# A new order of operations for a long-convolution block with a feed-forward network: FFN products between the first products of the inverse's second stage

## The chip, the cores and the metric

The kernel runs on one core of a Trainium2 chip. Its engines run side by side, each through a list of instructions of its own: TensorE (PE) multiplies matrices, VectorE (DVE) and ScalarE (ACT) work elementwise, GpSimd (POOL) and SyncE (SP) mostly issue transfers (DMA). The metric is the device time of one execution in microseconds; lower is better.

## The reference

With x of 2048 rows by 640 channels, xn is its layernorm. One branch multiplies a short convolution of k (four taps) by v, convolves the result along the rows with a filter as long as the sequence (by FFT, padded to 4096), adds a skip term and multiplies by xn. The other branch is a feed-forward network (FFN) with 1728 hidden units. Cut to what matters:

```python
kv = k_shift * v                                 # k_shift: 4-tap causal convolution of k
y = irfft(rfft(kv_pad) * rfft(kf_pad))[:S]       # long convolution, per channel
s = xn * (y + kv * ssm_D)
h = gelu(xn @ w1 + b1)                           # 640 -> 1728
g = silu(h @ w2 + b2)                            # 1728 -> 640
out = x + s * g
```

## The kernel before, in words

The FFTs are matrix products in two stages, and between the stages the data goes through DRAM to change which index lies across the partitions.

The program is a list of 713 named operations. A class `Plan` collects them, and `emit` issues them in the order of the string `ORDER` (from line 693). An engine runs its instructions in that order. A token such as `f2_14_1/N@6.0` names an operation (`f2_14_1`), optionally the engine or form (`/A` ACT, `/D` DVE, `/G` POOL, `/S` SP; `/N` splits each product in two of 64 columns), and the buffer slots it takes (`@6.0`: PSUM slot 6, then slot 0 of another pool). PSUM has eight slots. Semaphores between the engines follow from which memory an instruction reads and writes, one instruction at a time.

The names that matter here:

- `xl`, `Kl`, `w1l`, `w2l`, `kl`, `vl`: loads of x, the filter, the weights, k and v, on SP's queue. `wu`: warming products. `ws`: the sine tables.
- `bn`, `rs`, `xn`: layernorm of a tile of 128 rows. `xt` transposes it on PE, `xe` evicts it. `gt`, `gte` transpose the table for the end.
- `f1_c_r_ft`: first FFN product of row chunk c and block ft of the hidden layer (line 435), `ge_...` its Gelu on ACT (line 439). Block 13 is only half wide: `f1h_c` (line 450) and `geh_c` (line 456). `f2_i_h`: half h of the second product of tile i, fourteen products over the blocks in turn (line 476); tile 15 has three parts. It reads the chunk i // 4. `si_i` is its Silu (ACT, line 489), `gx_i` multiplies it into xn (DVE, line 493).
- `kv`: the short convolution and the product with v, on DVE (lines 522 to 531).
- `K1`, `K1r` and `U1`, `U1r`: first stage of the forward FFT of filter and data, `Ke`, `Ker`, `Ue`, `Uer` their evictions, `Ks`, `Us` the stores to DRAM (line 368), four of each.
- `KL`, `UL`: loads of the eight blocks of the second stage (lines 548, 550). `K2`, `U2`, `X2`: its products, `Kf`, `Uf` the evictions. `pr`, `pq`: products of the spectra on DVE. `i1`, `i1r`: first stage of the inverse (lines 604, 632), `ie`, `ir` its evictions, `cs` the store of a block (line 644).
- `cl_r`: load of a block for the inverse's second stage (line 656). It needs all eight `cs` to have landed. `i2_i`: its product for tile i (line 664). `ym_i` multiplies it into xn (DVE, line 668), `ad_i` adds x, `os_i` stores the tile.

Chunk 0 and 1 of the FFN run first, beside K1 and kv; f2 of tiles 0 to 7 beside U1; then f1 of chunks 3 and 2 beside the second stage and i1; f2 of tiles 8 to 11 around the end of i1; f2 of tiles 12 to 15 between the i2. Gelu and Silu need different tables on ACT, and `emit` puts a table load with a small probe (line 686) ahead of an activation whose table is not the one loaded.

Of the kernel before, what the change touches and what calls it, by code (L numbers as in the profile page):

```python
# [694 lines left out]
skl bn3 ws1 wu5@3 bn1 rs1 w1l3 K1_12@4.0 K1_13@6 K1_15@0 bn0 kl0 Ke_13/A wu3@2 ws0 xn2 wu1@3 rs0 xn3 Ke_12/A xt2@6.0  # L695
gt1@7 b1c xe2/D xt3@2 xn1 gt0@3 xe3/A xn0 xt1@6 sm1 xt0@4 xe1/A f1_0_1_1@5.0 xe0/D sm2 f1_0_1_0@2 bn4 f1_0_0_7@6
gte0/D ge_0_1_1 f1_0_0_8@4 bn5 ge_0_1_0 ge_0_0_7 Ke_15/A f1_0_1_2@5 bn7 f1_0_0_5@3 ge_0_1_2 gte1/D ge_0_0_8 one1 bn6
K1_4@0.2 ge_0_0_5 K1_5@6 f1_0_0_0@2 Ke_4/A Ke_5/D rs2 f1_0_0_6@5 ge_0_0_0 sm3 K1_6@0 ge_0_0_6 K1r_1@2 one0 Ke_6/D
# [1 line left out]
xt5@1.1 ge_0_1_4 f1_0_0_1@2 xe5/A xt4@3 kv0_1m@1 xt7@6 xt6@7 xe7/A f1_0_0_11@4 xe6/A kv0_1a f1_0_0_4@5 xe4/A  # L700
f1_0_1_3@1 ge_0_0_10 f1_1_0_5@6.1 ge_0_0_1 kv0_2m@1 ge_0_0_4 ge_0_1_3 K1_14@2 ge_1_0_5 K1r_3@0 kv0_2a f1h_1@7 Ke_14/A
f1_0_0_12/N@5 Ker_3/A bn12 f1_1_0_9/N@6 ge_0_0_11 Ks_3 bn13 vl0 ge_0_0_12 f1_1_0_8/N@2 w2l1 ge_1_0_9 vl1 kv0_3m@1 w2l0
geh_1 f1h_0@3 ge_1_0_8 K1_8@0.2 K1_10@4 kv0_3a K1_9@6 geh_0 f1_1_0_11@2 Ke_8/A bn14 f1_1_0_0@3 Ke_10/A bn15 f1_1_0_2@0
Ke_9/A Da rs4 K1_2@4.0 ge_1_0_2 K1_11@6 f1_0_0_3@1 Ke_11/D ge_1_0_0 f1_1_0_4@0 ge_1_0_11 kv1_1m@1 ge_0_0_3 K1r_0@6
ge_1_0_4 K1r_2@2 f1_1_0_10@1 Ker_2/A xn13 kv0_4 f1_1_0_6@0 Ks_2 ge_1_0_10 kl2 Ker_0/A f1_1_0_3@2 kv1_0@0 ge_1_0_6
f1_1_0_12@3 Ke_2/A kv1_1a ge_1_0_3 K1_1@6 K1_0@0 Ke_1/A K1_3@4 f1_1_0_7@2 kv1_2m@1 xl3 Ke_3/A f1_1_0_1@6 ge_1_0_12
kv1_2a f1_0_0_2@7 ge_1_0_1 f2_3_1@4.0 ge_1_0_7 xn12 kv1_3m@1 Ke_0/A ge_0_0_2 Ks_0 f2_3_0 kv1_3a kl3 vl3 vl2 kv1_4
U1_0@2.2 si_3 U1_1@0 f2_6_0@6.1 Ue_1/A gx_3 xn14 Ue_0/A kv2_0@1 U1_2@4 U1_3@0 Ue_2/A U1r_0@2 kv2_1m@0 f2_6_1 Ue_3/A
kv2_1a xt14@4.1 f2_1_0@0.0 xe14/A KL7@0 Uer_0/A kv2_2m@0 si_6 Us_0 U1_7@4.0 U1_5@2 KL2@1 kv2_2a Ue_7/A f2_1_1 KL1@4
Ue_5/A gx_6 kv2_3m@0 f2_0_0@6.1 si_1 KL0@2 kv2_3a U1_4@4 U1r_1@2 U1_6@0 Uer_1/A kv4_1m@0 f2_0_1 kv2_4 Ue_4/A xt12@2  # L710
si_0 xn15 xe12/D Ue_6/A kv4_0@1 kv4_1a Us_1 KL3@5 gx_0 f2_7_1@4.1 U1_8@6.2 U1_11@2 xt15@0 gx_1 xt13@1 xe15/D f2_7_0
xe13/A kv4_2m@0 Ue_8/A kv4_2a Ue_11/A f2_5_0@0.0 kv4_3m@0 si_7 kv4_3a ss gx_7 U1_10@6 kv4_4 U1r_2@2 Ue_10/A U1_9@4
f2_5_1 bn8 Ue_9/A kv3_0@0 Uer_2/A kv3_1m@1 K2_0_0@6 K2_1_0@4 si_5 Us_2 f2_2_0@2.1 kv3_1a Kf_0_0/A kv3_2m@1 Kf_1_0/A
kv3_2a U1_15@0.0 U1_14@6 Ue_15/A f2_2_1 kv3_3m@1 Ue_14/A kv3_3a kv3_4 f1_3_0_7@4.0 si_2 bn9 U1_12@0 U1_13@6 Ue_12/A
U1r_3@2 Ue_13/D f1_3_0_4@5 Uer_3/A bn11 K2_2_0@0 K2_3_0@6 Us_3 f1_3_0_5@2 bn10 f1_3_0_12@3 ge_3_0_4 Kf_2_0/D rs3
ge_3_0_7 f1_3_0_0@5 ge_3_0_5 ge_3_0_12 xn8 xn11 K2_7_0@0 ge_3_0_0 xt8@4.0 f1_3_0_9@2 Kf_3_0/A xe8/D xn9 K2_2_1@4 UL0@6
ge_3_0_9 xt11@3 Kf_2_1/D UL1@3 xt9@6 Kf_7_0/A UL2@8 f1_3_0_3@7 UL6@9 xe11/D UL3@10 xe9/D KL6@7 K2_0_1@4 ge_3_0_3
K2_1_1@0 xn10 K2_3_1@2 Kf_0_1/A xt10@6 Kf_3_1/D f1_3_0_1@7 Kf_1_1/A gx_2 K2_7_1@4 xe10/D X2_0@2 ge_3_0_1 gx_5 U2_0_0@0
Kf_0_2/A Kf_7_1/D f2_4_0@6.1 Uf_0_0/A Uf_0_2/D pq_0_1@2 U2_1_0@4 pq_0_0 U2_0_1@0 Uf_1_0/A f2_4_1 Uf_0_1/D sx/D
pr_0_0@3 U2_1_1@2 si_4 U2_2_0@4 X2_1@0 pr_0_1@0 Uf_1_1/A f1_2_0_6@6.1 Uf_2_0/D f1_2_0_11@7 UL4/G@2 Uf_1_2/D ge_2_0_6  # L720
i1_0@2.4 Kf_1_2/D ge_2_0_11 pq_1_0 f1_2_0_3@6 ie_0_0/A pq_1_1 pr_1_1@1 ie_0_1/A i1r_0@0.2 f1h_2@7 ir_1_0/D ir_0_1/A
ir_1_1/A pr_1_0@0 U2_2_1@4 ir_0_0/A X2_6@2 ge_2_0_3 U2_6_0@0 Uf_2_1/D Uf_6_2/A KL4@4 f1_2_0_0@6 Kf_6_2/A geh_2
pr_2_1@2 i1_1@2.4 Uf_6_0/A f1_2_0_10@7 ie_1_0/D ie_1_1/A U2_6_1@0 ge_2_0_0 X2_2@2 Uf_6_1/D ge_2_0_10 cs_1 U2_3_0@4
f1_2_0_9@6 Uf_3_0/A Kf_2_2/D Uf_2_2/D X2_4@0 ge_2_0_9 X2_3@4 pq_2_0@3 Kf_4_2/A pq_2_1 U2_3_1@2 Kf_3_2/A pr_2_0@0
f1_3_0_8@7 Uf_3_2/A Uf_3_1/A pq_3_1 f1_3_0_6@6 KL5@1 pq_3_0 Uf_4_2/A pr_3_0@1 ge_3_0_8 i1r_1@4.2 ge_3_0_6 K2_6_0@0
UL5/G@3 ir_3_0/D f1_2_0_2@7 ir_2_0/D ir_2_1/A ir_3_1/A pr_3_1@3 Kf_6_0/A i1_2@4.2 ge_2_0_2 UL7@5 f1_3_0_2@6 ie_2_0/D
ie_2_1/A K2_4_0@0 pq_4_1@0 U2_4_0@2 Kf_4_0/A K2_6_1@4 cs_2 Uf_4_0/D f1_2_0_4@7 Kf_6_1/A cs_0 i1_3@0.2 ge_3_0_2
pr_6_0@2 K2_4_1@4 ie_3_1/A f1_2_0_5@6 gx_4 Kf_4_1/D ie_3_0/A f1_3_0_11@2 ge_2_0_5 cs_3/S pr_6_1@1 ge_2_0_4 X2_5@0
ge_3_0_11 U2_4_1@4 Kf_5_2/D K2_5_0@6 Uf_4_1/A f1_2_0_8@3 Uf_5_2/D Kf_5_0/A pq_5_1 i1_6@0.4 pr_4_0@3 ge_2_0_8
f1_2_0_1@2 ie_6_1/A ie_6_0/D U2_7_0@6 ge_2_0_1 pq_5_0 U2_5_0@4 K2_5_1@0 pq_4_0 Uf_5_0/A f1_2_0_7@3 pr_4_1@1 Kf_5_1/A  # L730
f1_2_0_12@2 Uf_7_0/D ge_2_0_7 i1r_2@4.0 ge_2_0_12 pq_6_0@2 U2_7_1@6 ir_4_1/D ir_4_0/A X2_7@2 ir_5_0/A ir_5_1/D
Uf_7_1/A i1_4@4.0 Kf_7_2/D pq_6_1 Uf_7_2/A f2_11_0@6.0 ie_4_1/A pq_7_1 pq_7_0 pr_7_0@0 ie_4_0/A U2_5_1@2 cs_4/S
pr_7_1@1 i1r_3@0.4 Uf_5_1/A f2_11_1 ir_6_0/A pr_5_0@3 ir_7_0/A ir_7_1/D i1_7@2.0 ir_6_1/D si_11 pr_5_1@2 cs_6/S
# [47 lines left out]
```

## Time and profile before

| | |
|---|---|
| median of 3 runs | 183.24 us (182.97 to 183.44) |
| the profiled execution | 184.05 us, span 182.3 us |
| PE, DVE, ACT, POOL busy | 175.0, 160.9, 138.5, 22.6 us |
| ACT table loads for Gelu and Silu | 8, 10.3 us |
| DMA | 50.64 MB, mean 278 GB/s |

The span runs from the program's first instruction to its last; the rest of the execution's time lies around it. A row of the timeline or of the chain begins with its start and its length in us; then come engine, line, operation, out<-in and the number of instructions taken together, and in brackets the idle time before it and what ended it. PEld is the loading of weights into PE, SPq an issue in SP's queue.

### The profile page before, as it was taken

The numbers are of one execution on the slowest core, as the hardware profiler recorded it, in microseconds if no ns is written. First come the engines' busy times: TensorE is split into PE (matmuls) and PEld (weight loads), VectorE is DVE, ScalarE is ACT, GpSimd is POOL, SyncE is SP. The second block draws the span as 40 slices with busy tenths as digits, with TensorE's granted clock in tenths as the row PEclk, the third lists the DMA queues.
The fourth block names the chain that finished last, engine by engine and source line by source line (L and its number), as shares of the span: only waits on it lengthen the run. The fifth ranks groups of instructions, "written<-read, shape, count | busy, mean of one in ns | idle before, by whom it ended". The sixth has DMA issues, their size and how long they took to land.

```text
span 182.3 us, 5182 instructions
## 1 busy us (share of the span) xinstructions
PE 175.0 (96%) x2192; PEld 99.9 (55%) x2192; DVE 160.9 (88%) x252; ACT 138.5 (76%) x201; POOL 22.6 (12%) x52
## 2 busy tenths in 40 slices
...
GB/s 187 411 415 403 199 367 407 334 425 432 409 309 403 417 358 397 153 287 76 222 340 367 172 141 158 148 325 377 148 4 88 206 287 132 416 405 392 66 189 144
DMA packets 19417, 50.64 MB, mean 278 GB/s; under 512 B 1729, under 2 KB 13506, under 8 KB 17986
## 3 DMA queue, kind: packets, MB, share of 16 engines
...
## 4 chain that ended last, share of the span: by engine, by line
PE 81%; DVE 8%; ACT 7%; issue 1%; ACTq 0%; DVEq 0%
PE ps L435 30%; PE ps L476 30%; PE ps L349 4%; PE ps L604 4%; PE ps L563 4%; PE ps L413 3%; PE ps L664 2%; DVE xn L668 2%; ACT v L181 2%; DVE stats L381 2%; ACT L686 1%; ACT k L181 1%; PE ps L360 1%; PE ps L450 1%; DVE w L238 1%
## 5 line engine op out<-in xcount | busy, mean ns | idle before, releaser
L476 PE MATMUL ps<-w,hT 128*64 128x320 bf16 (+4 forms) x644 | 65.0, 293 | 0.0
L435 PE MATMUL ps<-xnT,w 128*128 128x512 bf16 (+2 forms) x300 | 61.2, 362 | 0.5 <-ACT sl L489 0.2
L476 PEld LDWEIGHTS <-hT 128*64 128x64 bf16 (+3 forms) x644 | 45.3, 105 | 17.4 <-issue 3.9
L435 PEld LDWEIGHTS <-w 128*128 128x128 bf16 (+1 forms) x300 | 26.4, 99 | 28.5 <-issue 6.2
L181 ACT CAST st<-ps 128x1024 bf16<-128x1024 f32 x36 | 35.0, 1014 | 3.4 <-PE ps L360 1.8
L439 ACT ACTIVATE hT<-ps,b1f 128x512 bf16<-128x512 f32 (+1 forms) x57 | 35.0, 665 | 1.2 <-PE ps L435 1.0
L489 ACT ACTIVATE sl<-ps 128x640 bf16<-128x640 f32 (+2 forms) x18 | 11.6, 647 | 24.0 <-PE ps L476 19.4
L529 DVE TENSOR_TENSOR lat<-lat 128x2560 bf16<-128x2560 bf16 (+1 forms) x15 | 18.4, 1225 | 0.5
L526 DVE TENSOR_TENSOR lat<-k,lat 128x2560 bf16<-128x2560 bf16 (+1 forms) x15 | 18.3, 1218 | 0.2
L181 ACT CAST k<-ps 128x1024 bf16<-128x1024 f32 (+2 forms) x19 | 16.2, 878 | 2.6 <-PE ps L563 1.5
L181 ACT CAST v<-ps 128x1024 bf16<-128x1024 f32 (+2 forms) x18 | 14.5, 839 | 0.4 <-PE ps L563 0.4
L668 DVE TENSOR_TENSOR xn<-ps,xn 128x640 bf16<-128x640 f32 x16 | 12.6, 819 | 2.2 <-PE ps L664 2.0
L493 DVE TENSOR_TENSOR xn<-xn,sl 128x640 bf16<-128x640 bf16 (+2 forms) x18 | 8.0, 448 | 7.3 <-ACT sl L489 7.2
L181 DVE CAST k<-ps 128x1024 bf16<-128x1024 f32 (+2 forms) x14 | 11.8, 857 | 2.3 <-PE ps L563 0.9
L381 DVE BATCH_NORM_STATS2 stats<-x 128x6 f32<-128x320 bf16 x32 | 13.7, 470 | 0.0
L686 ACT ACT_TABLE_LOAD x8 | 10.3, 1283 | 0.1
L396 POOL TENSOR_SCALAR rstd<-mv 128x4 f32<-128x4 f32 (+1 forms) x5 | 1.3, 257 | 69.2 <-DVE mv L382 69.2
L181 ACT CAST lat<-ps 128x1024 bf16<-128x1024 f32 (+2 forms) x12 | 9.4, 826 | 0.2 <-PE ps L604 0.2
L604 PE MATMUL ps<-st,I 32*64 32x512 bf16 x256 | 8.8, 380 | 0.1
L332 PE MATMUL ps<-hT 128*128 128x512 bf16 x24 | 7.5, 477 | 1.2 <-DVE mhalf L212 1.2
L181 DVE CAST lat<-ps 128x1024 bf16<-128x1024 f32 (+2 forms) x9 | 7.9, 892 | 0.7 <-PE ps L604 0.3
L181 ACT COPY xnT<-ps 128x640 bf16<-128x640 bf16 x8 | 5.3, 695 | 3.9 <-PE ps L413 3.9
...
## 6 DMA issues: line engine op xcount, KB each, us to landing
...
w<-in_w SPq DMA_DIRECT2D x2, 1120.0 KB, 10.3
...
```

Source lines behind the costliest of these rows:

```text
L181: (nc.scalar.copy if e == "ACT" else nc.vector.tensor_copy)(out=out_, in_=in_)
L381: nc.vector.bn_stats(out=stats[:, i, h, :], in_=x_t[:, i, h * H:(h + 1) * H])
L435: nc.tensor.matmul(out=pb.v[us, 0:b - a], lhsT=w1_t[:, ft, t, us], rhs=xnTb[c].v[:, a // P:b // P, t, :], start=(t == 0), stop=(t == DT - 1))
L439: nc.scalar.activation(out=hTb[c].v[:, ft, a:b], in_=pb.v[:, 0:b - a], func=ACT.Gelu_apprx_tanh, bias=b1_f[:, ft:ft + 1], scale=1.0)
L476: nc.tensor.matmul(out=o[us, 0:b - a], lhsT=hTb[c].v[0:M, ft, q * P + us.start:q * P + us.stop], rhs=w2_t[0:M, ft, a:b], start=(ft == 0), ...
L489: nc.scalar.activation(out=o_, in_=i_, func=ACT.Silu)
L493: op("gx_" + nm, "DVE", lambda e, a=a, b=b: nc.vector.tensor_tensor(out=xn_t[:, i, a:b], in0=xn_t[:, i, a:b], in1=s_.v[:, a:b], op=ALU.mul ...
L526: op("kv%d_%dm" % (r, j), "DVE", lambda e, i=i, n=n, j=j, t=t, wb=wb: nc.vector.tensor_tensor(out=t.v[:, 0:n, :], in0=k_t[:, i + 3 - j:i + ...
L529: op("kv%d_%da" % (r, j), "DVE", lambda e, n=n, t=t, a=a: nc.vector.tensor_tensor(out=a.v[:, 0:n, :], in0=a.v[:, 0:n, :], in1=t.v[:, 0:n, ...
L604: nc.tensor.matmul(out=pb[j // 2].v[64 * a:64 * a + 64, j % 2, :], lhsT=I1_t[32 * j:32 * j + 32, m, :], rhs=o[w][32 * j:32 * j + 32, a, r, ...
L668: op("ym_%d" % i, "DVE", lambda e, i=i, pb=pb: nc.vector.tensor_tensor(out=xn_t[:, i, :], in0=pb.v.rearrange("p a b -> p (a b)")[:, 0:D], ...
L686: nc.scalar.activation(out=tab[:], in_=cst[:], func=func)
```

## The change

Only the string `ORDER` changes; the 713 operations are the same. Nearly every operation stands at another place among those of other engines, many take other PSUM slots, and some fifty change their engine, nearly all evictions between ACT and DVE (such as Ke_5, Ke_11 to ACT and Ke_3 to DVE) and transfers between SP, POOL and ACT (cl_2 and cl_4 to POOL, cl_1 to SP, cs_0 to SP, cs_3 to POOL). Split products (`/N`) are now f1_0_1_2, f1_1_0_11, f1_1_0_12 in place of f1_0_0_12, f1_1_0_8, f1_1_0_9, and f2_8_0, f2_8_1 and f2_9_0 are split no longer.

PE's part from the end of the inverse's first stage, before and after:

```
before: i1_7 f1_3_0_10 i1_5 f2_10_0 f2_10_1 f1h_3 f2_8_1/N f2_8_0/N f2_9_0/N i2_1 i2_0 f2_9_1/N i2_5 i2_4 f2_14_1/N
        i2_3 i2_2 i2_10 f2_14_0/N i2_11 i2_14 f2_12_1/N ...
after:  i1_7 f2_8_1 i1_5 f2_8_0 f2_10_1 f2_10_0 f2_9_0 f1_3_0_10 f1_3_0_11 i2_0 f2_9_1/N i2_3 i2_1 f1h_3 i2_5 f2_14_0/N
        i2_2 i2_4 i2_11 f2_14_1/N i2_8 i2_10 f2_12_0/N ...
```

ACT's Gelu and Silu there: before `si_10 si_8 | ge_3_0_10 geh_3 | si_9 si_14`, after `si_8 si_10 | ge_3_0_10 ge_3_0_11 | si_9 | geh_3 | si_14`, with a table load at each bar. The third part of f2's last tile, f2_15_2, which was PE's last operation, now stands ahead of i2_6.

The core of the diff: the start, the rows around the K stores, and the end.

```diff
-b1l/A grid xl1 zz c0 xl0 wu2@0 fix wm0 wm2/G Kl4 w1l0 wm1 xl2 w1l2 wu4@1 wq0 Kl1 wq1 w1l1 sm0 Kl2 wq2 wu0@2 bn2 ws2 id
+b1l/A grid xl1 zz c0 xl0 wu2@0 fix wm0 wm2/G Kl4 xl2 wm1 w1l1 w1l0 wu0@1 wq0 w1l2 wq1 w1l3 ws0 id Kl2 wq2 wu4@2 bn2
...
-K1_7@6 Ker_1/A f1_0_0_9@4 xl4 Kl0 xn4 Dl/A kl1 f1_0_1_4@5 xn5 Ke_7/A Kl3 xn7 f1_0_0_10@0 xn6 ge_0_0_9 kv0_0@0 Ks_1
+ge_0_0_6 xn5 K1r_1@2 K1_7@0 xt5@5.1 Ke_4/A xl4 f1_0_0_11@4 xe5/D Kl3 xn6 vl0 Ker_1/A xn7 Kl0 f1_0_0_3@5 xn4 xt6@6
+kv0_1m@0 ge_0_0_3 xt7@7 xt4@2 xe6/A f1_0_0_10@3 xe7/A kv0_0@1 xe4/A f1h_0@5 ge_0_0_10 f1_1_0_11/N@6.1 ge_0_0_11 kv0_1a
+geh_0 f1_0_1_2/N@7 f1h_1@2 Ke_7/A kv0_2m@0 f1_1_0_12/N@3 ge_0_1_2 Ks_1 ge_1_0_11 K1r_3@4 kv0_2a K1_14@0 Ker_3/A
...
-f1_3_0_10@4 ie_7_1/A ie_7_0/D i1_5@6.0 cs_7/S f2_10_0@2.1 ie_5_0/A ie_5_1/D gx_11 cs_5/S f2_10_1 f1h_3@5 si_10
-f2_8_1/N@6.0 cl_0@8 gx_10 cl_2@6 cl_1/G@10 cl_5/G@4 f2_8_0/N cl_7/G@7 cl_3/G@0 f2_9_0/N@0.1 cl_6/G@1 si_8 gx_8 i2_1@2
-i2_0@6 ge_3_0_10 ym_1 f2_9_1/N geh_3 ad_1 ym_0 i2_5@2 ad_0 i2_4@4 ym_5 f2_14_1/N@6.0 si_9 os_0 os_1 ym_4 cl_4@2 ad_4
+ir_6_1/A Uf_5_1/A cs_6/S gx_5 ir_7_1/D ir_7_0/D pr_5_1@1 i1_7@4.0 si_11 f2_8_1@6.1 pr_5_0@3 ie_7_0/A ie_7_1/A gx_11
+i1_5@2.4 cs_7/S f2_8_0 ie_5_0/D ie_5_1/A cs_5/S f2_10_1@0.0 si_8 gx_8 f2_10_0 cl_0@5 cl_1@10 cl_2/G@9 f2_9_0@4.1
+cl_5/G@4 si_10 cl_4/G@6 gx_10 cl_7/G@2 f1_3_0_10@2 cl_6/G@0 f1_3_0_11@3 ge_3_0_10 cl_3/G@3 i2_0@6 ge_3_0_11 f2_9_1/N
+ym_0 ad_0 os_0 i2_3@0 si_9 i2_1@2 ym_3 f1h_3@6 i2_5@4 ym_1 ad_3 geh_3 f2_14_0/N@0.0 ym_5 os_3 ad_5 i2_2@2 i2_4@6
```

More of the change, by code (lines that the diff above doesn't have):

```diff
@@ L693 @@
 ORDER = """
-b1l/A grid xl1 zz c0 xl0 wu2@0 fix wm0 wm2/G Kl4 w1l0 wm1 xl2 w1l2 wu4@1 wq0 Kl1 wq1 w1l1 sm0 Kl2 wq2 wu0@2 bn2 ws2 id
[L695 to L698, printed above, removed]
@@ L699 @@
-K1_7@6 Ker_1/A f1_0_0_9@4 xl4 Kl0 xn4 Dl/A kl1 f1_0_1_4@5 xn5 Ke_7/A Kl3 xn7 f1_0_0_10@0 xn6 ge_0_0_9 kv0_0@0 Ks_1
[L700 to L733, printed above, removed]
```

45 lines of the change are left out of this document (40 added, 5 removed).

## The prediction

> **What bounds the kernel now.** I read the page's head first, then busy time by stage, the chain that ended last, and the timeline of the last 40 us with its DMA issues.
>
> ```profile
> span 182.3 us, 5182 instructions
> PE 175.0 (96%) x2192; PEld 99.9 (55%) x2192; DVE 160.9 (88%) x252; ACT 138.5 (76%) x201; POOL 22.6 (12%) x52
> ```
>
> That is the page. By stage (PE, PEld, DVE, ACT, POOL busy, clock, DMA share, GB/s):
>
> ```profile
> 10.02:48.00 37.98, 37.87 (x305) 21.07 (x306) 35.80 (x59) 35.93 (x56) 8.20 (x22) 1.00 0.97 374
> ...
> 95.37:145.25 49.88, 49.30 (x962) 23.44 (x948) 46.74 (x63) 46.68 (x70) 4.07 (x5) 1.00 0.59 196
> 145.25:156.04 10.79, 10.37 (x131) 7.86 (x123) 2.61 (x4) 3.92 (x6) 2.67 (x5) 1.00 0.70 225
> 156.04:178.59 22.55, 21.92 (x344) 17.25 (x344) 21.05 (x39) 6.42 (x11) 0.00 (x0) 1.00 0.73 283
> ```
>
> PE is busy nearly throughout, and between 10 and 48 and between 95 and 145 DVE and ACT are nearly full too. The third row shown is different: DVE is busy 2.61 of 10.79 us and ACT 3.92. It runs from the end of i1_5, the last first-stage product of the inverse, to the first i2. What happens in it:
>
> ```profile
> 144.22 1.10 PE L604 MATMUL ps<-st,I 32*64 32x512 bf16 x32
> 145.44 1.22 DVE L181 CAST k<-ps 128x1024 bf16<-128x1024 f32 x1 [0.65 <-PE ps L604]
> 146.76 0.36 SPq L644 DMA_DIRECT2D scrC<-k  x1
> 151.62 0.33 SPq L656 DMA_DIRECT2D lat<-scrC  x1
> 156.04 0.41 PEld L664 LDWEIGHTS <-G 128*64 128x64 bf16 x8 [0.75 <-DMA lat<-scrC]
> ```
>
> i1_5 is evicted (145.44 + 1.22), its block is written out (cs_5, issued 146.76), all blocks must have landed, cl_0 is issued at 151.62, and i2 begins at 156.04. From PE's leaving i1_5 (145.25) that is 10.8 us of two transfers one after the other, whatever PE does meanwhile. So the end is made of three pieces: when i1_5 is done, these 10.8 us, and what follows the first i2 (156.04 to 182.3). Work that PE does inside the 10.8 us costs nothing as long as it fits; work ahead of i1_5 and behind the first i2 counts.
>
> **The change part by part.** The execution shown took 184.05 us, of which 182.3 are its span and 1.75 lie around it; the median of the runs is 183.24, 0.81 lower. I work out a difference in this span and take it off the median.
>
> ```profile
> 48.14 3.81 PE ps L476 x28
> 114.97 2.26 PE ps L435 x10
> 149.23 0.67 PE ps L450 x10
> 167.94 1.90 PE ps L476 x28
> 169.84 0.27 PE ps L664 x4
> ```
>
> These are the prices on PE: half an f2 tile 1.90 (two unsplit halves 3.81; one half split into 28 products 1.90, so that taking the /N split off f2_8_0, f2_8_1 and f2_9_0 and moving it among the f1 costs nothing), an f1 1.13, f1h 0.57 to 0.67, an i2 0.27.
>
> *The start.* gt0, gt1 and the warming wu3 move among the transposes.
>
> ```profile
> 2.08 0.43 SPq L304 DMA_DIRECT2D w<-in_w  x1
> 10.02 0.45 PE L413 MATMUL ps<-ident,xn 128*128 128x128 bf16 x5 [0.35 <-DVE xn L403]
> 12.13 2.55 PE L435 MATMUL ps<-xnT,w 128*128 128x256 bf16 x16
> ...
> w<-in_w SPq DMA_DIRECT2D x1, 320.0 KB, 5.7
> ```
>
> The first transpose (10.02) is released by xn2, and the DVE chain up to it (bn2, bn3, bn1, bn0) stays as it is. wu3, four products, falls into the wait for Ke_12 and xn0, which the old order spends at the same place on gt0 and gt1. Taken as 0; at most its own four products. The weights w1l0 now go out behind xl2 and w1l1, 1.1 MB later: at the 398 GB/s of a full stretch (the row stands with the last rival) 2.8 us after the 2.08 + 5.7 of today, 10.6, and the first f1 wants them at 12.13.
>
> *Ahead of i1_5.* f2_8_1 comes in (1.90), f1_3_0_10 and f1_3_0_11 go out (2.26). Taking for every product the shortest spacing of its kind in this trace, 129.9 us of spacing lie between the first f1 and the end of i1_5 in the old order and 129.45 in the new one; the difference of 0.1 beyond 1.90 - 2.26 is one change fewer between full and narrow products. Term: -0.45. In the trace the same stretch took 133.1 (12.13 to 145.25), so 3.2 us are waits of PE, most of 0.1 to 0.3 us. The largest stands here:
>
> ```profile
> 98.23 1.01 ACT k L181
> 99.27 1.18 ACT L686
> 100.76 0.60 ACT sl L489
> 101.40 2.32 PE ps L435 x10
> 104.81 2.19 ACT v L181 x3
> ```
>
> ACT evicts Uf_1_0, loads the Silu table, runs si_4, and f1_2_0_6 waited for the PSUM that Uf and si give back. The new order puts both f1 ahead of X2_1, so this wait (0.3) has cover. But i1r_0 waits for the eviction ie_0_0 (104.81 + 1.01 = 105.8) on ACT, 7.6 us after Uf_1_0 began, and ACT's sequence between them is unchanged; so what is won at f1 is waited for at i1r_0. Behind that 12 evictions go from DVE to ACT and 12 from ACT to DVE; with ge_3_0_11 gone, the busy time of each up to i1_5, counted by its groups' means, changes by about 0.1 us. I keep the 3.2 us of waits as they are: 0, with bounds of -1.0 (the 1.1 us of them that come before U2_0_0 vanish nearly all) and +1.0 (a third more).
>
> *DVE ahead of Us_3.* Up to kv3_4 DVE loses two K evictions, gte1, xe2, xe12, xe15 and bn8 and takes Ke_3, xe1, xe5, b1c and sx, some 3 us less.
>
> ```profile
> 81.79 0.83 DVE L531 TENSOR_TENSOR v<-lat,v 128x1280 bf16<-128x1280 bf16 x1
> 82.77 0.61 PE L349 MATMUL ps<-v,W 64*128 64x512 bf16 x4
> ```
>
> Today U1_12 follows kv3_4 at once (82.62, 82.77). Earlier values help Us_3 and the loads behind it, but U2_0_0 comes when PE has finished the products before it, so 0 is taken.
>
> *The 10.8 us.* PE's work in them is now f2_8_0, f2_10_1, f2_10_0, f2_9_0, f1_3_0_10, f1_3_0_11: 4 x 1.90 + 2.26 = 9.9. It fits. cs_7 gets a little more room before cs_5 (f2_8_1 of 1.90 stands between their products where an f1 stood): -0.1, from -0.4 to +0.1.
>
> *Behind the first i2.* f1h_3 has moved here (+0.57). In the old order PE waited once, for cl_5:
>
> ```profile
> 160.96 0.71 PE L664 MATMUL ps<-lat,G 128*64 128x512 bf16 x8
> 162.30 0.14 PEld L664 LDWEIGHTS <-G 128*64 128x64 bf16 x4 [0.95 <-DMA v<-scrC]
> 162.31 0.46 PE L664 MATMUL ps<-v,G 128*64 128x512 bf16 x4 [0.63 <-DVE xn L668]
> ```
>
> i2_3 and i2_2 began at 160.96, so by the price of an i2 PE was through at 161.5; i2_10 began at 162.31: 0.8 of waiting. The new order wants that block only after f2_14_0, some 6.2 us behind the first i2, about when it landed (162.3 is 6.3 behind): -0.8. The later blocks, in their new queue places (cl_4 leaves SP, where it stood behind two stores, for POOL), come 1.7 us apart (0.655 MB at the 389 GB/s of that stretch) and are wanted later than that:
>
> ```profile
> 156.04:169.30 13.26, 12.63 (x184) 9.64 (x186) 12.00 (x20) 4.27 (x7) 0.00 (x0) 1.00 0.98 389
> ```
>
> New is a wait for the Gelu of f1h_3:
>
> ```profile
> 153.80 0.70 ACT L489 ACTIVATE sl<-ps 128x640 bf16<-128x640 f32 x1 [3.83 <-PE ps L476]
> 154.52 1.28 ACT L686 ACT_TABLE_LOAD   x1
> 155.82 0.20 ACT L686 ACTIVATE tab<-cst 128x1 f32<-128x1 f32 x1
> 155.93 0.67 ACT L439 ACTIVATE hT<-ps,b1f 128x512 bf16<-128x512 f32 x1
> 156.49 0.94 ACT L456 ACTIVATE hT<-ps,b1f 64x256 bf16<-64x256 f32 x2
> ```
>
> geh_3 now stands between si_9 and si_14, which makes two table loads more, 2 x 1.48 us of ACT. The second lies in ACT's idle time. The first is on the path: with T the start of i2_0, f2_9_1 ends at T+2.4, si_9 (0.7) at T+3.15, table and probe (1.48) at T+4.6, geh_3 (0.94) at T+5.55. PE reaches f2_14_0 at T+3.6. Only its last products, the 14th block of the hidden layer, read what geh_3 writes; they come 26/28 x 1.90 = 1.77 later, at T+5.4. So it waits 0.2: +0.2. On DVE the 41 operations of the tail are the same. Sum: 0.57 - 0.8 + 0.2 = 0, from -0.2 to +0.6.
>
> Against this stands the Trainium skill, "ScalarE: Activation LUTs", section "What ACT_TABLE_LOAD costs": it counts a drain of about 1.38 us to each load of 1.28 us. This trace shows the 1.28 but no drain: 0.01 between load and probe. By the page geh_3 would end near T+6.9 and the sum would be 1.4 us higher.
>
> Of the 0.3 ahead of f1_2_0_6 I take 0.1 as won. Total: -0.45 - 0.1 - 0.1 + 0 = -0.65: **182.6**, span 181.65.
>
> **The rivals.** *Waits only change place.* PE's 3.2 us of waits come from three engines that are full together; 0.45 us less work ahead of i1_5 is then paid in waits: 183.2. For it: i1r_0 above. Chance 0.19.
>
> *f2_14_0 waits as a whole* (slower). If its first product and not its last waits for geh_3, PE stands from T+3.6 to T+5.55, 1.75 more than counted, and DVE, without ym_2, with it: 184.4. It decides as soon as the wait sits on a product before the 26th. The old order has geh_3 done at 157.4, well ahead of its first reader, and shows neither. Chance 0.12.
>
> *Table switch dearer than its row.* A pause of another 1.28 us behind the load moves geh_3 to T+6.8: 183.9. The rows above speak against it. Chance 0.04; this stands in for the page's drain.
>
> *SP's queue held by Ks_1* (slower). Ke_7 moves behind geh_0, whose f1h_0 PE reaches at about 23.9 by the spacing count, so to about 26, and with it Ks_1, which is issued at 22.16 today; Ks_3, w2l1, kl2, w2l0, vl1 and Kl1 are queued behind it.
>
> ```profile
> 22.16 0.43 SPq L368 DMA_DIRECT2D scrK<-st  x1
> 30.49:45.27 14.78, 14.67 (x106) 6.65 (x102) 13.77 (x20) 14.56 (x23) 1.31 (x2) 1.00 1.01 398
> ```
>
> At 398 GB/s the 5.8 MB from the remainder of Ks_1 to Kl1 take 14.6 us from 30.5: 45. K1r_0 reads Kl1 near 48.6, f2_3_0 reads w2l0 near 46.6. If the stretch slips by more than 3.5 us, PE waits for each further one: 1 to 2 us, 183.6 to 184.6. Chance 0.12. Another 0.03 is for something unseen on the slow side.
>
> **How the numbers follow.** The forecast has 0.50, with a range of its own of 181.4 to 183.4 (-1.0 and +1.0 of waits, hand-over and tail bounds not all at once); 0.42 of it lies beyond 0.3% (0.55 us, about what a measurement of this kernel can tell), below 182.69, and 0.08 within. The unchanged rival gives 0.03 faster and 0.16 same. The three slow ones and the unseen make 0.31. Faster 0.45, same 0.24, slower 0.31. The range reaches down to 181.4 and up to 184.6, which takes in the slow rivals.
>
> **What would show it.** In the profile after: i1_5's products about 0.4 us earlier; 10.5 to 10.9 us from there to the first i2, with PE idle for about 0.5 to 1 ahead of it; ten table loads; f2_14_0 starting about 3.6 us after the first i2 with a pause of 0.2 in its last products; no i2 waiting for DMA by more than 0.3; 22.5 us from first i2 to the last product. Wrong, if i1_5 is late by more than 0.5 us, or if PE pauses by a microsecond ahead of f2_14_0 or K1r_0.

## The result and the profile after

The kernel after takes **184.12 us** (median of 8 runs, 184.01 to 185.17) where the kernel before takes 183.24 (182.97 to 183.44): a ratio of 1.0058, 95% interval 1.0039 to 1.0077, so slower by 0.9 us by the medians and 1.1 by the ratio. The profiled execution of after took 184.12 us for a span of 182.2. The prediction was 182.6.

The head of the page of after:

```profile
span 182.2 us, 5097 instructions
PE 175.6 (96%) x2150; PEld 100.1 (55%) x2150; DVE 156.3 (86%) x249; ACT 145.3 (80%) x209; POOL 25.8 (14%) x52
```

The span is 0.1 shorter than the one that the prediction read (182.3), and yet the time is 0.9 above the median of before. That is the first thing to clear up; the table by stages and a second profile of before do it. Busy time by stage of after, cut at the first X2 or U2, the end of i1_5, the first i2 and the last product (columns PE, PEld, DVE, ACT, POOL, clock, DMA share, GB/s):

```profile
95.00:145.37 50.37, 49.44 (x968) 24.24 (x951) 45.34 (x63) 47.47 (x70) 4.08 (x5) 1.00 0.57 186
145.37:155.26 9.89, 9.89 (x75) 6.37 (x67) 2.21 (x3) 4.59 (x6) 3.05 (x6) 1.00 0.69 232
155.26:177.75 22.49, 22.49 (x355) 17.67 (x354) 20.55 (x39) 9.43 (x15) 0.14 (x1) 1.00 0.77 289
177.75:182.20 4.45, 0.00 (x1) 0.00 (x0) 0.77 (x3) 0.30 (x1) 0.00 (x0) 0.84 0.31 102
```

The same view of a second profiled execution of before (183.12 us, span 181.3; the first experiment below):

```profile
95.38:145.28 49.90, 49.32 (x962) 23.43 (x948) 46.75 (x63) 46.71 (x70) 4.08 (x5) 1.00 0.59 196
145.28:155.86 10.58, 10.37 (x131) 7.87 (x123) 2.61 (x4) 3.72 (x5) 2.68 (x5) 1.00 0.69 225
155.86:177.59 21.73, 21.73 (x344) 17.54 (x344) 20.88 (x39) 6.64 (x12) 0.00 (x0) 1.00 0.77 296
177.59:181.30 3.71, 0.00 (x0) 0.00 (x0) 0.64 (x3) 0.30 (x1) 0.00 (x0) 0.84 0.42 132
```

Read by rows: i1_5 ends 0.09 later in after (the first X2 or U2 comes 0.38 earlier, and the stage behind it takes 0.47 longer); the hand-over, from i1_5's end to the first i2, is 0.69 shorter; from the first i2 to the last product it takes 0.76 longer; and from the last product to the end 0.74 longer (4.45 against 3.71; 0.82 with the spans' ends unrounded). Together 0.09 - 0.69 + 0.76 + 0.82 = 0.98, which is the 0.99 between the two spans. Two of the terms belong together: in the hand-over PE is busy for 9.89 of 9.89 us in after and for 10.37 of 10.58 in before. So 0.48 of the 0.69 is work, f1h_3 above all, that comes back behind the first i2; only 0.21 is a wait that is gone.

The hand-over of after, row by row of the timeline:

```profile
144.37 1.07 PE L604 MATMUL ps<-st,I 32*64 32x512 bf16 x32
145.48 1.23 DVE L181 CAST k<-ps 128x1024 bf16<-128x1024 f32 x1 [1.43 <-PE ps L604]
147.15 0.36 SPq L644 DMA_DIRECT2D scrC<-k  x1
151.28 0.33 SPq L656 DMA_DIRECT2D v<-scrC  x1
155.26 0.46 PE L664 MATMUL ps<-v,G 128*64 128x512 bf16 x4
```

cs_5 is issued 0.4 later than in before and its block lands earlier, so that cl_0 goes out at 151.28 instead of 151.62; cl_0 lands at 155.21 in the trace, and PE, busy for all 9.89 us, gets to it at 155.26. Behind the first i2:

```profile
158.00 0.71 PE L450 MATMUL ps<-xnT,w 128*64 128x256 bf16 x10
158.39 1.28 ACT L686 ACT_TABLE_LOAD   x1
158.94 2.17 PE L476 MATMUL ps<-w,hT 128*64 128x320 bf16 x28
159.68 0.20 ACT L686 ACTIVATE tab<-cst 128x1 f32<-128x1 f32 x1
159.79 0.94 ACT L456 ACTIVATE hT<-ps,b1f 64x256 bf16<-64x256 f32 x2
160.94 0.71 PE L664 MATMUL ps<-lat,G 128*64 128x512 bf16 x8
```

f2_14_0 starts at 158.94, 3.68 behind the first i2, and hands over to i2_2 at 160.94: 2.00 for a half that costs 1.90, so geh_3 delays it by 0.1. Between load and probe there is 0.01, as in before.

The last stores of after, first the elementwise end and the two queues in the timeline, then the same issues by tile (duration in ns min/median/max):

```profile
177.47 1.98 SPq L651 DMA_DIRECT2D out<-x  x2
178.07 0.90 ACTq L651 DMA_DIRECT2D out<-x  x1
178.41 0.24 DVE L680 TENSOR_TENSOR x<-xn,x 128x160 bf16<-128x160 bf16 x1
...
179.06 0.38 SPq L651 DMA_DIRECT2D out<-x  x1
```

```profile
L651 SPq DMA_DIRECT2D out<-x x3: 332/384/1500, 176.7 to 179.1; - x3
L651 ACTq DMA_DIRECT2D out<-x x2: 339/620/902, 177.1 to 178.1; - x2
```

One issue of SP, os_8 at 177.47, takes 1.50 us where others take 0.33, and one of ACT 0.90. os_15_1 has its data at 178.65 and stands behind os_8 until 179.06. In the DMA view of 177.0 to 178.8 of the same execution a fetch of program stands beside them, and the stores land late:

```profile
q8 instruction: 1, 0.02, 4.8%
...
out<-x ACTq DMA_DIRECT2D x1, 160.0 KB, 2.9
out<-x SPq DMA_DIRECT2D x1, 160.0 KB, 3.2
```

The trace has that fetch, 16 KB, from 177.20 to 178.60. In the second profile of before, where the last fetch begins at 175.3, the last stores land within 1.7 (DMA view of 176.7 to 181.2):

```profile
out<-x ACTq DMA_DIRECT2D x1, 80.0 KB, 1.7
out<-x SPq DMA_DIRECT2D x1, 40.0 KB, 1.7
out<-x ACTq DMA_DIRECT2D x1, 40.0 KB, 1.6
```

The prediction has no term for this.

### The profile page after: what moved, and what is told of

The parts are those of the page before. It is cut to its first block, busy times and chain, and to the rows that moved or that the text cites. A ratio compares the mean times of both kernels' runs of the same rounds, so it can differ in the third digit from the quotient of the medians.

```text
span 182.2 us, 5097 instructions
## 1 busy us (share of the span) xinstructions
PE 175.6 (96%) x2150; PEld 100.1 (55%) x2150; DVE 156.3 (86%) x249; ACT 145.3 (80%) x209; POOL 25.8 (14%) x52
## 5 line engine op out<-in xcount | busy, mean ns | idle before, releaser
L476 PE MATMUL ps<-w,hT 128*128 128x320 bf16 (+4 forms) x602 | 65.5, 293 | 0.0
L435 PE MATMUL ps<-xnT,w 128*128 128x512 bf16 (+3 forms) x300 | 61.1, 360 | 0.1
L476 PEld LDWEIGHTS <-hT 128*128 128x128 bf16 (+2 forms) x602 | 44.5, 103 | 19.1 <-issue 4.7
L181 ACT CAST k<-ps 128x1024 bf16<-128x1024 f32 (+2 forms) x21 | 17.6, 871 | 1.5 <-PE ps L604 1.0
L181 ACT CAST v<-ps 128x1024 bf16<-128x1024 f32 (+2 forms) x15 | 12.5, 868 | 1.7 <-PE ps L563 1.0
L181 DVE CAST k<-ps 128x1024 bf16<-128x1024 f32 (+2 forms) x12 | 10.0, 842 | 3.9 <-PE ps L604 1.4
L181 ACT CAST lat<-ps 128x1024 bf16<-128x1024 f32 (+2 forms) x15 | 12.4, 849 | 0.8 <-PE ps L563 0.7
L396 POOL TENSOR_SCALAR rstd<-mv 128x4 f32<-128x4 f32 (+1 forms) x5 | 2.3, 456 | 67.4 <-DVE mv L382 67.4
L181 DVE CAST lat<-ps 128x1024 bf16<-128x1024 f32 (+2 forms) x13 | 10.6, 827 | 0.7 <-PE ps L604 0.3
L403 DVE TENSOR_SCALAR xn<-x,mv,rstd 128x640 bf16<-128x640 bf16 x16 | 6.8, 462 | 1.5 <-POOL rstd L397 1.5
```

The source lines that it names most:

```text
L181: (nc.scalar.copy if e == "ACT" else nc.vector.tensor_copy)(out=out_, in_=in_)
L435: nc.tensor.matmul(out=pb.v[us, 0:b - a], lhsT=w1_t[:, ft, t, us], rhs=xnTb[c].v[:, a // P:b // P, t, :], start=(t == 0), stop=(t == DT - 1))
L476: nc.tensor.matmul(out=o[us, 0:b - a], lhsT=hTb[c].v[0:M, ft, q * P + us.start:q * P + us.stop], rhs=w2_t[0:M, ft, a:b], start=(ft == 0), ...
```

## The experiments

The theories of this section are A (the profile that the prediction read had waits of its own), B (the program fetch at the end makes the loss; E is its rival in before), C and D (a loss ahead of i1_5, or between the i2), F and G (which engine sets the pace ahead of i1_5: PE, or ACT and DVE), and H, J and K (three guesses at what to exchange there). All ratios are to before on the same chip, since the median of before is 183.24 to 183.88 from chip to chip.

**before_again.** No edit.

> The kernel before, unchanged, profiled a second time. Theory A (the profiled execution of before was 0.81 us above the median because of waits that ordinary executions lack: the 0.75 us of PE ahead of the first i2 and the 0.8 us ahead of i2_10): span near 181.5, first i2 within 10.2 us of the end of i1_5 or no wait of PE for cl_5, last product at about 177.8. Rival: the same two waits stand in this trace too and the span is again 182.2 to 182.4; then the 0.81 us lie around the span.

The median of ten runs is 183.48, 1.0000 of before (0.9984 to 1.0016); the profiled one took 183.12, with a span of 181.3. The two traces of before agree within 0.04 us from the first f1 to the end of i1_5. Then:

```profile
155.86 0.73 PE L664 MATMUL ps<-lat,G 128*64 128x512 bf16 x8 [0.21 <-DMA lat<-scrC]
...
161.32 0.44 PE L664 MATMUL ps<-v,G 128*64 128x512 bf16 x4
```

The first i2 is 0.18 earlier, and i2_10 follows i2_2 without the 0.8 of waiting for cl_5: 161.32 instead of 162.31. So theory A holds for cl_5, and of the hand-over's wait only 0.2 went. How much such waits take varies: single runs of before lie between 182.9 and 185.1 over the chips used. That the median runs lack the wait for cl_5 is inferred from this one profile.

**after_unsplit and after_split56.** PE's program gets shorter or longer by 30 and 56 instructions, and with it the place of its fetches moves.

```diff
-f1_1_0_11/N  f1_0_1_2/N  f1_1_0_12/N        (after_unsplit)
+f1_1_0_11    f1_0_1_2    f1_1_0_12
-f2_6_0    f2_6_1                            (after_split56)
+f2_6_0/N  f2_6_1/N
```

> The kernel after, with f1_0_1_2, f1_1_0_11 and f1_1_0_12 no longer split: 15 products fewer at 25 us, at the same time on PE (1.07 us each way). Theory B (in after, a fetch of 16 KB of program that begins at 177.2 and takes 1.4 us holds back the stores: the issue of os_8 takes 1.50 us instead of 0.33, and os_15_1 behind it goes out at 179.06 though its data is ready at 178.65): 30 instructions fewer on PE move that fetch 0.6 us later or past the end; if it is gone, the last issues take 0.33 us each, the span shrinks by 0.4 to 0.7 and the time is 183.4 to 183.7; if it comes at 177.8 it holds the very last stores, 184.1 to 184.6. Rival C (the time was lost ahead of the first i2, in the stage of the inverse's first products): 184.1, same within 0.1, wherever the fetch falls.

> The kernel after, with f2_6_0 and f2_6_1 split in two of 64 columns: 28 products (56 PE instructions) more at 52 us, at the same time on PE. Theory B: 112 products of the tail take 4.8 us, so 56 instructions move the last fetch 1.2 us earlier, to 176.0; the stores held are then not the last ones, and the time is 183.4 to 183.8. Rival C: 184.1, within 0.1.

after_unsplit: 183.55 us, 1.0008 (0.9996 to 1.0020), with no fetch behind 172, all last issues at 0.33, and 2.8 us from the last elementwise operation to the end. That is what theory B expected. It might be 0.3 better still, had the edit been free: PE is 0.34 later from 28 us on, 0.10 to 0.12 at each of three more changes between narrow products (f1h is always split) and full ones. after_split56: 183.93, 1.0020 (1.0008 to 1.0032), above the 183.4 to 183.8 that B gave. Its fetch begins at 176.17 and its end is 2.8 us long, as B had it; but the product ahead of U2_0_0 waited for a block (PE idle for 0.42, what follows 0.6 later), and two more changes cost 0.2.

**ahead_btail.** After through cs_5, then before's order of the rest.

```diff
 ... i1_5@2.4 cs_7/S f2_8_0 ie_5_0/D ie_5_1/A cs_5/S
-f2_10_1@0.0 si_8 gx_8 f2_10_0 cl_0@5 ...
+f1_3_0_11@2 ge_3_0_11 f1_3_0_10@4 f2_10_0@2.0 f2_10_1 f1h_3@5 si_10 cl_0@8 ...
```

> After's order through cs_5, then what is left in the order of before (f1_3_0_11 and f1_3_0_10 first, as f2_8_1 is done; the split f2_8_0 and f2_9_0 are back, 28 products more). Theory B (after's first part costs nothing, its end does, by the fetch): 183.0 to 183.5, with the last store's issue at 0.34. Rival C (the loss lies ahead of i1_5): 184.0 or more. Rival D (the new order between the i2 itself is worse, by geh_3 and the order of the blocks): 183.0 to 183.3, with a fetch near the end all the same.

183.69, 1.0015 (1.0001 to 1.0028): a little above the ranges of B and D. (Of the split halves only f2_9_0 is back, f2_8_0 stays whole: 14 products more than in after and not 28.) i1_5's end at 145.37, first i2 at 155.88, last product at 177.61: with before's end 0.6 of the shorter hand-over is gone (10.51, with f1h_3 in it and PE busy throughout), and so is the 0.76 behind it (21.73); 3.1 us lie behind the last elementwise operation.

**before_fetch.** The counterpart: before with as many PE instructions as after.

```diff
-f2_8_1/N@6.0 ... f2_8_0/N ... f2_9_0/N@0.1
+f2_8_1@6.0 ... f2_8_0 ... f2_9_0@0.1
```

> The kernel before with f2_8_0, f2_8_1 and f2_9_0 no longer split: 42 products (84 PE instructions) fewer, as many as the change took away, and nothing else moved. Theory B (a program fetch beside the last stores costs 0.8 us at the end): the last fetch, at 175.27 in the second profile of before, moves 1.8 us later to about 177.1, half a microsecond ahead of the last product, where after has it; from the last elementwise operation to the span's end 3.4 to 3.6 us instead of 2.78, and the time 0.5 to 0.9 above before. Rival E (the fetch is harmless in before, whose last stores go out on ACT's queue too): 0 to 0.2 above before, for two more changes between narrow and full products, with 2.8 us at the end.

184.43, **1.0040** (1.0019 to 1.0061), within B's range, with 3.5 us behind the last elementwise operation. Its timeline and the DMA view of 177.8 to 179.5:

```profile
178.25 1.36 SPq L651 DMA_DIRECT2D out<-x  x1
178.49 1.62 ACTq L651 DMA_DIRECT2D out<-x  x2
```

```profile
q8 instruction: 1, 0.02, 4.4%
```

With the fetch there, at 178.04 in that execution, before's own last stores are late. The end alone is 0.74 longer than in the second profile of before. The rest of this profile's longer span lies in the hand-over, where the first i2 waited 0.8 for cl_0 (0.21 there); whether the edit made that wait is open, so the ratio alone does not size the fetch.

**after_tailfull.** The fetch taken away from after at the smallest price: the last three halves unsplit.

```diff
-f2_13_1/N ... f2_15_0/N@2 ... f2_15_1/N
+f2_13_1 ... f2_15_0@2 ... f2_15_1
```

> The kernel after with the last full-width f2 halves, f2_13_1, f2_15_0 and f2_15_1, no longer split: 42 products (84 PE instructions) fewer, all behind the last i2, at the price of one change from narrow to full products (0.1). Theory B: PE's instructions end before the place that calls the last fetch; no fetch after 172, last issues of 0.33 each, 2.8 us from the last elementwise operation to the end instead of 3.6; span 181.4 to 181.6, time 0.7 below after, so 0.997 to 1.000 of before. Rival C: 1.004 to 1.006 of before, as after.

183.61, **0.9995** (0.9978 to 1.0011): as B has it, with a span of 181.7, a little above the 181.4 to 181.6 expected. Its last stores, and the DMA view from 172 on, in which no fetch stands:

```profile
178.32 0.34 ACTq L651 DMA_DIRECT2D out<-x  x1
178.66 0.24 DVE L680 TENSOR_TENSOR x<-xn,x 128x160 bf16<-128x160 bf16 x1
...
178.93 0.33 SPq L651 DMA_DIRECT2D out<-x  x1
```

```profile
q1 hardware_dynamic: 1296, 1.23, 37.4%
q10 hardware_dynamic: 288, 0.25, 7.6%
...
out<-x SPq DMA_DIRECT2D x7, 160.0 KB, 1.9
```

**after_again.** No edit, on the chip of after_evict, after_gx4 and after_both.

> The kernel after, unchanged, on the chip of the three kernels beside it. Theory B: a fetch of 16 KB begins at 177.1 to 177.3 again, 3.5 to 3.6 us from the last elementwise operation to the span's end, and 0.6 to 0.8 us above the kernels that end without it. Rival: the fetch's place or length was an accident of one execution; then this one ends in 2.8 us and its median is that of the kernel with unsplit halves at the end.

184.18, 1.0042 (1.0021 to 1.0064), the fetch at 177.78 and 3.4 us at the end. The nine profiles together:

| kernel | last fetch begins | last elementwise ends | span | between |
|---|---|---|---|---|
| before, before again | 176.9, 175.3 | 179.5, 178.5 | 182.3, 181.3 | 2.8, 2.8 |
| after, after again | 177.2, 177.8 | 178.7, 178.9 | 182.2, 182.3 | 3.6, 3.4 |
| before_fetch | 178.0 | 179.2 | 182.7 | 3.5 |
| ahead_btail | 176.8 | 178.5 | 181.6 | 3.1 |
| after_split56 | 176.2 | 179.5 | 182.3 | 2.8 |
| after_unsplit, after_tailfull | none | 179.0, 178.9 | 181.8, 181.7 | 2.8, 2.8 |

Where the fetch begins 2.5 us or more ahead of the last elementwise operation's end, or there is none, the end takes 2.8 us; where it begins 1.1 to 1.5 us ahead, 3.4 to 3.6; ahead_btail, 1.7 ahead, lies between. The other eleven profiles agree: in before_swap the last fetch begins 3.2 us ahead, in the others by 173.4 at the latest, and all eleven end in 2.8.

**after_geh.** After_tailfull with f1h_3 and its Gelu ahead of the pair of table loads.

```diff
-f1_3_0_11@3 ge_3_0_10 ... i2_0@6 ge_3_0_11 f2_9_1/N ... i2_1@2 ym_3 f1h_3@6 i2_5@4 ym_1 ad_3 geh_3
+f1_3_0_11@3 f1h_3@6 ge_3_0_10 ... i2_0@0 ge_3_0_11 geh_3 f2_9_1/N ... i2_1@2 ym_3 i2_5@4 ym_1 ad_3
```

> As the kernel with the three unsplit halves at the end, and f1h_3 moved ahead of the first i2 (behind f1_3_0_11) with geh_3 behind ge_3_0_11, ahead of si_9: two table loads fewer, no wait of f2_14_0 for geh_3. If the block that the first i2 reads has landed by 155.3 (in after PE reaches the first i2 at 155.26 without a wait): first i2 at 155.8, 21.8 us from there to the last product instead of 22.5, PE's end 0.2 earlier than in that kernel; eight table loads. Rival: the work only fills a place in which PE would have been waiting, then 0.5 earlier; or the earlier blocks are not there yet when the i2 come sooner behind the first: no gain, 0 to 0.3 later.

183.88, 1.0012 (0.9998 to 1.0026): no gain. From the first i2 to the last product it still takes 22.6:

```profile
156.23:178.81 22.58, 22.00 (x306) 18.79 (x302) 20.57 (x39) 6.09 (x11) 0.00 (x0) 1.00 0.72 275
```

```profile
158.94 0.70 ACT L489 ACTIVATE sl<-ps 128x640 bf16<-128x640 f32 x1
159.69 0.46 PE L664 MATMUL ps<-lat,G 128*64 128x512 bf16 x4 [0.57 <-ACT sl L489]
```

i2_5 takes the PSUM that si_9 gives back, and si_9 stands behind a table load. In after, f1h_3 (0.65) lay over that wait. Neither the expectation nor its rivals named it.

**before_swap.** The change's exchange ahead of i1_5 alone, in before; the Gelus and some PSUM slots move with it, and f2_8_1 stays split.

```diff
-f1_3_0_11@2 ge_2_0_5 ... i1_7@2.0 ... f1_3_0_10@4 ie_7_1/A ie_7_0/D i1_5@6.0 cs_7/S f2_10_0@2.1 ... f2_10_1 f1h_3@5 ... f2_8_1/N@6.0
+ge_2_0_5 ... i1_7@2.0 si_11 f2_8_1/N@6.1 ... ie_7_1/A ie_7_0/D gx_11 i1_5@4.0 cs_7/S f2_10_0@2.0 ... f2_10_1 f1_3_0_10@4 f1_3_0_11@5 f1h_3@0
```

> The change's one part alone, in the kernel before: f2_8_1 ahead of i1_5, and f1_3_0_10 and f1_3_0_11 behind it (between f2_10_1 and f1h_3, their Gelus and geh_3 on ACT before si_8). PE has 0.36 us less ahead of i1_5 (1.90 in, 2.26 out). Theory F (PE sets the pace there, as the prediction's step had it): i1_5 ends 0.3 to 0.4 earlier than the 145.28 of before, first i2 and end with it, 0.998 of before. Rival G (ACT and DVE set it; work that leaves PE comes back as waits): i1_5's end within 0.1 of 145.28, and 0.999 to 1.001 of before.

184.05, 1.0021 (1.0001 to 1.0041): worse than F and G both had it. From the first f1 to the end of i1_5:

```profile
12.77:147.02 134.25, 132.57 (x1681) 70.88 (x1679) 126.34 (x177) 120.36 (x173) 12.39 (x25) 1.00 0.76 280
```

134.25 against before's 133.15 (12.13 to 145.28). In the trace X2_5 comes 0.48 earlier once f1_3_0_11 (1.09) is out, and by f1_2_0_8, 1 us on, nothing of it is left; f2_8_1 in place of f1_3_0_10 then counts in full (0.73), with 0.4 of waits besides. This profile took 185.08, 1.03 above the kernel's median; 0.64 of that is a later first f1, so up to 0.4 of the 1.1 may belong to this execution alone.

**after_evict, after_gx4, after_both.** Guesses at where the waits of after come from.

```diff
-ir_1_0/A ir_0_1/D ir_1_1/D Uf_2_2/A Kf_2_2/A Uf_3_0/D Uf_6_1/A ... ie_5_0/D ie_5_1/A   (after_evict: 24 of them)
+ir_1_0/D ir_0_1/A ir_1_1/A Uf_2_2/D Kf_2_2/D Uf_3_0/A Uf_6_1/D ... ie_5_0/A ie_5_1/D
-si_4 f1_2_0_11@6.1 Uf_1_1/A gx_4 ... ge_2_0_5 pr_6_0@0                                 (after_gx4)
+si_4 f1_2_0_11@6.1 Uf_1_1/A ... ge_2_0_5 gx_4 pr_6_0@0
```

> As the kernel with the unsplit halves at the end, and the 24 evictions behind U2_0_0 that the change moved between ACT and DVE back on the engine of before (order unchanged). Theory H (these exchanges made the 0.7 us more of PE's waits between U2_0_0 and the end of i1_5): i1_5 ends 0.4 to 0.7 earlier than the 145.38 of that kernel, time 0.996 to 0.998 of before. Rival G (ACT and DVE are both full there, and the order of PE's products against them is what costs): within 0.15 of 145.38 or later, time as that kernel.

> As the kernel with the unsplit halves at the end, and gx_4 back from DVE's place at 101.7 (behind si_4) to its place in before, behind the Gelu of f1_2_0_5. Theory J (its 0.48 us stand in DVE's row ahead of pq_1_1 and pr_1_1, on which i1r_0 and i1_1 wait): the wait of 0.3 at i1r_0 goes, i1_5 ends 0.3 to 0.5 earlier than 145.38, and with it first i2 and end; 0.997 of before. Rival G: ACT, without a pause from 101 to 125, holds i1_1 and i1r_1 all the same; i1_5's end within 0.1.

> Both at once: gx_4 and the 24 evictions as in before. Theories H and J together: i1_5's end 0.6 to 0.9 earlier than 145.38, time 0.995 of before. Rival G: no more than the better of the two alone.

186.66 (1.0163), 183.90 (1.0029), 186.75 (1.0176): i1_5's end 2.9, 0.4 and 2.9 later than in after_tailfull. H and J are refuted as they stood. That the engines were chosen for the order they stand in would explain it, but was not tested: the 24 evictions were moved at once.

**less_pe, less_act, less_dve.** Work is left out of one engine between i1_1 and i1_2, on after_tailfull.

```diff
-for t in range(DT):                                    (less_pe)
+for t in range(1 if nm in ("3_0_8", "3_0_6") else DT):
-hT[:, ft, a:b] = gelu(ps[:, 0:b - a])                  (less_act)
+hT[:, ft, a:a + 64], for nm in ("3_0_8", "2_0_0", "2_0_10", "2_0_9")
-evict(B[:, ri::2, 0:512], ps)                          (less_dve)
+evict(B[:, ri::2, 0:64], ps[:, :, 0:64]), for U2_2_1 and U2_3_0
```

> As the kernel with the unsplit halves at the end (i1_2 at 120.05, i1_5's end at 145.38), but f1_3_0_8 and f1_3_0_6 make one product each in place of five: 1.7 us of PE's work left out at 111 and 117. Theory F (PE sets the pace between U2_0_0 and the end of i1_5): i1_2 and i1_5's end 1.5 to 1.7 earlier. Rival G (ACT and DVE set it, and work that leaves PE comes back as waits): i1_2 0 to 0.5 earlier, i1_5's end 0 to 0.4.

> As that kernel, but the Gelus of f1_3_0_8, f1_2_0_0, f1_2_0_10 and f1_2_0_9 (0.7 us each, at 113 to 117) work on 64 of 512 columns: some 1.6 us of ACT's work left out. If ACT sets the pace there: i1_2 0.5 to 1.0 earlier, i1_5's end 0.3 to 0.8. Theory F: 0 to 0.2.

> As that kernel, but the evictions Uf_2_1 and Uf_3_0 on DVE (1.22 us each, at 108.5 and 112.6) work on 64 of 512 columns: some 2.0 us of DVE's work left out. If DVE sets the pace there: i1_2 0.5 to 1.0 earlier, i1_5's end 0.3 to 0.8. Theory F: 0 to 0.2.

Each is a single execution. Busy time in the 15 us from 105 (105.57 in less_pe, whose first f1 came 0.57 later) and from the first f1 to the end of i1_5; after_tailfull, then less_pe, less_act, less_dve:

```profile
105.00:120.00 15.00, 14.34 (x324) 6.63 (x322) 14.15 (x21) 14.94 (x27) 1.09 (x2) 1.00 0.82 261
12.22:145.38 133.16, 132.21 (x1667) 70.98 (x1665) 122.11 (x177) 122.41 (x176) 14.83 (x26) 1.00 0.78 281
```

```profile
105.57:120.57 15.00, 12.69 (x316) 6.07 (x314) 14.24 (x21) 14.94 (x27) 1.07 (x2) 1.00 0.83 265
12.79:145.94 133.15, 130.53 (x1659) 70.41 (x1657) 122.28 (x177) 122.72 (x176) 14.51 (x25) 1.00 0.78 281
```

```profile
12.22:145.05 132.83, 132.08 (x1668) 70.83 (x1665) 121.94 (x177) 121.36 (x176) 14.83 (x26) 1.00 0.79 281
```

```profile
12.22:145.35 133.13, 132.20 (x1667) 70.97 (x1665) 120.44 (x177) 122.63 (x176) 14.80 (x26) 1.00 0.79 282
```

With PE 1.65 us less busy in the 15 us, i1_5 ends after the same 133.15: **F is refuted**. With DVE 1.67 less busy (122.11 to 120.44) it ends 0.03 earlier. Of the three only ACT's work counts: 1.05 less (122.41 to 121.36), and 0.33 earlier. In the 15 us ACT is busy 14.94.

**bhead_atail.** Before through cs_5, then after's order of the rest, with the unsplit end.

```diff
 ... i1_5@6.0 cs_7/S f2_10_0@2.1 ie_5_0/A ie_5_1/D gx_11 cs_5/S
-f2_10_1 f1h_3@5 si_10 f2_8_1/N@6.0 cl_0@8 ...
+f2_8_1@6.0 f2_8_0 f2_10_1 si_8 gx_8 cl_0@5 ...
```

> Before's order through cs_5, then what is left in the order of after, with the three unsplit halves at the end. By the terms measured so far: i1_5's end at 145.28 as in before; the hand-over 9.9 as in after (PE has 9.5 us of work in it), first i2 at 155.2; 22.6 us from there to the last product, 177.8; 3.7 to the end, span 181.5, time 183.2 to 183.4 with little spread, 0.999 of before. Rival: the hand-over keeps before's 10.4 to 10.8, because its blocks are stored later; then 183.8 to 184.2.

186.12, 1.0131 (1.0098 to 1.0165): far off. The first i2 comes 11.0 behind i1_5's end (PE waits 1.3 for its block), and the later i2 wait for PSUM from other ym than in after, since the joined order needed other slots. So the expected sum of the two parts did not come about; on either part alone this run says nothing.

**after_uf32 and after_kf22.** One eviction from ACT to DVE, on after_tailfull.

```diff
-Uf_3_2/A          (after_uf32)        -Kf_2_2/A          (after_kf22)
+Uf_3_2/D                              +Kf_2_2/D
```

> As the kernel with the unsplit halves at the end, and the eviction Uf_3_2 (0.59 us on ACT at 113.8) on DVE, which pauses 0.33 and 0.42 us at 112.5 and 117.5. Theory K (ACT, without a pause from 101 to 118, sets when i1r_1 starts, and so i1_5): i1r_1 and i1_5's end 0.3 earlier, as where 1.6 us of Gelus were left out there (0.33); the end 0.3 to 0.4 earlier, 0.997 to 0.999 of before: the best version. Rival: DVE's row, 0.68 longer, takes the place of ACT's: 0 to 0.3 later.

> As that, but with Kf_2_2 (0.59 us on ACT at 111.2) on DVE in place of Uf_3_2. Theory K: i1r_1 0.3 earlier and the end with it. Rival: it stands in DVE's row ahead of ie_1_0 and Uf_3_0, which give back PSUM and feed the products of the next block: 0.1 to 0.6 later.

183.70, 1.0005 (0.9984 to 1.0027), and 183.54, 0.9977 (0.9956 to 0.9998). K is not borne out: in after_uf32 i1_5 ends 0.17 later by the first f1 (133.33), and in after_kf22 i1r_1 comes 0.17 earlier by the first f1, and by the end of i1_5 0.04 of it is left (133.12). Its ratio is the lowest of all and below 1 by its interval, but its interval overlaps that of after_tailfull, from which its trace differs by no more than that.

## Why the prediction was wrong

*The range.* 184.12 lies inside the stated range, but only because that takes in the slow rivals, and none of the three that it names is what happened: SP's queue was not held (PE is busy 82.75 of 82.78 us from the first f1 to the first X2 or U2), f2_14_0 waited 0.1, and no pause follows a table load. Three steps failed: the waits ahead of i1_5, the wait for cl_5, and what splitting a product costs. A fourth, the hand-over, was sized wrong.

*What it was taken off.* The prediction worked out a difference in a span of 182.3 and took it off a median that belonged to a span of about 181.4 (183.24 less 1.8). It said that the execution lay 0.81 above the median, and left it there. By before_again the 0.81 was the wait for cl_5: without that wait the span is 181.3. The term "-0.8 (no wait for cl_5)" removed a wait that the median, by that profile, did not hold.

*The start, 0.* The first f1 comes at 12.22 instead of 12.13: +0.09. Right within what it claimed; SP's queue held nothing up.

*Ahead of i1_5, -0.45 and -0.1.* Here is the mechanism that failed. The step counted PE's work and kept PE's 3.2 us of waits as they were. The work did shrink, by its count of spacings 0.45 (PE's busy time in the stretch falls from 132.39 to 132.19); from the first f1 to the end of i1_5 both kernels take 133.15 (12.13 to 145.28, 12.22 to 145.37), so waits took all 0.45 and the 0.1. The rival "waits only change place" had this, with a chance of 0.19. less_pe bears it out: 1.7 us less of PE's work there does nothing. ACT, busy 14.94 of 15 us, counts: 1.05 us less of its work gave 0.33. Which chain it is in full stays open; none of the five kernels that exchanged evictions or gx_4 shortened it by more than 0.04.

*The hand-over, -0.1.* It became 0.4 to 0.9 shorter: 9.89 and 10.16 in two profiles of after, 10.79 and 10.58 in two of before. That PE's 9.9 us of work fit was right, that PE would stand for 0.5 to 1 us ahead of the first i2 was wrong. The step was mis-sized: it held the transfers at 10.8, and they took less than PE's 9.9 (cs_5 4.0 us from issue to landing against 4.7). Why was not tried. The room that the prediction named is there: cs_7 goes out 2.5 us ahead of cs_5, against 1.9. A program fetch seems to count here, too: one stands beside cs_5 in after and in before, and in after_unsplit, whose fetch comes only at 150.46, cs_5 lands in 3.3 and cl_0 goes out 5.18 behind i1_5's end instead of 5.91. Even so the first i2 comes 9.90 behind it: in after's order PE's own work sets the hand-over.

*Behind the first i2, 0.* Of 0.57 - 0.8 + 0.2 the first and the last are right in sum: 0.57 + 0.2 = 0.77, and 22.49 - 21.73 = 0.76 (f1h_3 0.65, f2_14_0's wait 0.1). The middle term was void, as said. "22.5 us from first i2 to last product" came to 22.49, but that is no gain: it holds against the 22.55 of the profile with the wait, and not against the 21.73 of the one without. f2_14_0 at 3.68 behind the first i2 and the ten table loads came as said, the dear table switch and the wait of f2_14_0 as a whole did not.

*Behind the last product.* No step covered it. It is the largest term of the loss: 0.6 to 0.8 us, by a fetch that stands beside the last stores. 42 products fewer moved it from 175.3 (second profile of before; 176.9 in the first, with a later end) to 177.2 and 177.8. Nor did the list of what would make the prediction wrong look there: neither i1_5 nor a pause ahead of f2_14_0 or K1r_0 was at fault. The prediction took splitting a half as free because it costs PE nothing (1.90 either way). It changes the number of PE's instructions, and so where the fetches fall: that is the step's failure. Without the fetch the change is worth nothing measurable (0.9995); with it, 0.4 to 0.6%.

Summed by what was measured, from the start to the end: 0.09 + 0 - 0.69 + 0.76 + 0.82 = 0.98, against -0.65.
